# A decode step with cached attention and an MLP on one core: three w4 pieces behind the last V, three wo buffers, the residual put into the accumulator

## The chip, the cores and the metric

The kernel runs on one core of a Trainium2 chip. The core has five engines with their own instruction queues: TensorE (PE, with its weight loads shown as PEld), VectorE (DVE), ScalarE (ACT), GpSimd (POOL) and SyncE (SP), which here issues nearly all loads. Sixteen DMA engines carry each load together. The metric is the device time of one execution in microseconds, the median of three runs. All times below are microseconds (us) unless marked ns; times within the profile count from the start of its span.

## The reference, cut to what matters

One token for each of four sequences passes through two branches that share a layernorm, and both are added to the input:

```
xn  = layernorm(x)                                 # x: 4 x 1 x 576
A   = softmax(q k^T / sqrt(128)) v, then @ wo      # q = xn @ wq, 32 heads of 128;
                                                   # 16 KV heads, the last 2048 of 8192 positions
h   = gelu(layernorm(xn) @ w1), shifted by tokens, @ w2
x1  = xn + that                                    # S = 1: the shifts leave only zeros
B   = x1 + gelu(layernorm(x1) @ w3) @ w4           # w3: 576 x 4608, w4: 4608 x 576
out = x + A + B
```

With one token each shift moves the only row out, so w1 and w2 drop out and x1 is xn. The result is `x + xn + attention @ wo + gelu(...) @ w4`, 4 rows of 576 numbers in bf16. The core has to read 16 K heads and 16 V heads (2 MB each), wq, wo, w3 and w4: 87.17 MB in all.

## The kernel before, in words

**The stages.** First the queries are computed from wq and laid out in `qz`. Then a loop over the 16 K heads (`k_scores`, L251): DVE transposes the head in two instructions (L257), PE multiplies (L266). Beside the first five heads run the pieces of w3 (`g_piece`, L375); then `gelu` makes `gT`, 36 chunks of activations. `softmax` (L272) makes the exponentials `E`, the scaled rows `pr` and their transposes `PZ`. Then a loop over the 16 V heads: `v_compute` (L318) is 64 matmuls on one head, `head_out` (L341) copies the result (`on`, L346) and leaves two things for later: `select` (four small matmuls, L350, and two copies `onx`, L358), and for every second head `project`, which multiplies with one wo tile.

**The accumulator.** `ACC` is one PSUM bank, zeroed at the start by DVE (L180). Columns 0 to 287 gather the sum of all wo and w4 products; the 576 output columns are folded in two halves that stand in partitions 0 to 3 and 32 to 35. `acc_matmuls` (L327) adds one chunk as a pair of matmuls, one for each half. A wo tile is 4 such pairs, a w4 piece of 9 rows is 9 pairs. Columns 320 to 463 hold the w3 product. At the end one DVE instruction adds `xres`, the residual x + xn in the same fold, and casts (`fin`, L458); two small DMAs, on SP's and ACT's queue, write the output (L460).

**What sets the order.** Tiles come from pools with a fixed number of buffers, and a load waits until the buffer's last reader is done: 6 buffers for K and V heads (`kv`), 3 for wq, w3 and w4 (`w`), 2 for wo. All loads stand on SP's queue in the order of the program, so a load that waits holds up every load behind it. A load also waits for the transfer eight places ahead of it to land, since there are eight semaphores for transfers in turn. SP's order after K15, where w4(e, i) is the piece of half e that starts at chunk i:

```
before: w4(0,0) V0 wo0 w4(0,9) V1 w4(1,0) V2 wo1 V3 V4 wo2 V5 V6 wo3 ... V13 V14 wo7 V15 w4(1,9) in 4, 2, 2, 1
```

Each wo tile from wo2 on waits for a projection that frees its buffer (wo2 for that of wo0). On PE the three w4 pieces loaded early are multiplied before, within and after the softmax; the last one, w4(1,9), is split in loads of 4, 2, 2 and 1 chunks, and its products come after V15's.

Of the kernel before, what the change touches and what calls it, by code (L numbers as in the profile page):

```python
# [9 lines left out]
ALU = mybir.AluOpType  # L10
AX = mybir.AxisListType
BF16 = mybir.dt.bfloat16
F32 = mybir.dt.float32
# [8 lines left out]
def kernel(  # L22
# [18 lines left out]
    nc = tc.nc  # L41
    P = 128
    B, Sq, D = A_x.shape
    _, Hkv, Sk, Dh = A_k_cache.shape
# [7 lines left out]
    NCH = W // G  # L52
    NG = P // G
    GK = G // B
# [8 lines left out]
    DH = D // 2  # L63
# [19 lines left out]
    const = ctx.enter_context(tc.tile_pool(name="const", bufs=1))  # L83
# [2 lines left out]
    ktp = ctx.enter_context(tc.tile_pool(name="kt", bufs=2))  # L86
    pzp = ctx.enter_context(tc.tile_pool(name="pz", bufs=1))
    wpl = ctx.enter_context(tc.tile_pool(name="w", bufs=NWP))
    wop = ctx.enter_context(tc.tile_pool(name="wo", bufs=2))
    ps_tp = ctx.enter_context(tc.tile_pool(name="ps_tp", bufs=1, space=PSUM))  # L90
    ps_s = ctx.enter_context(tc.tile_pool(name="ps_s", bufs=4, space=PSUM))
    ps_o = ctx.enter_context(tc.tile_pool(name="ps_o", bufs=2, space=PSUM))
# [34 lines left out]
    ident = const.tile([P, P], BF16)  # L127
# [27 lines left out]
    def transposed_pe(prep):  # L155
        src_bf, dup, T = prep
        tp = ps_tp.tile([P, KJ + 2, B], BF16, tag="tp")
        for j in range(KJ):
            nc.tensor.transpose(out=tp[:, j, :], in_=src_bf[:, j:KJ * P:KJ], identity=ident[0:B, 0:B])
        for e in range(2):  # L160
            nc.tensor.transpose(out=tp[:, KJ + e, :], in_=dup[:, e, :], identity=ident[0:B, 0:B])
        nc.vector.tensor_copy(out=T[:], in_=tp[:])
# [14 lines left out]
        nc.vector.memset(qz_f[:, i * nq:(i + 1) * nq], 0.0)  # L177

    ACC = ps_acc.tile([P, 512], F32)
    nc.vector.memset(ACC[:], 0.0)  # L180
    GP0 = 320
    gp = ACC[:, GP0:GP0 + NF * B].rearrange("p (f b) -> p f b", b=B)
    gT = const.tile([P, NF, B], BF16)
# [39 lines left out]
    for y in range(NY):  # L223
        tq = ps_o.tile([P, 2 * HB, P], BF16, tag="O", name=f"tq{y}")
        for k in range(2):
            for m in range(HB):
                nc.tensor.transpose(out=tq[:, k * HB + m, :],
                                    in_=q_rows[:, k, m, y, :, :].rearrange("p g i -> p (g i)"), identity=ident[:])
# [11 lines left out]
    ln2T = ln2_prep[2]  # L240
    xsum = const.tile([B, D], F32)
    nc.vector.tensor_tensor(out=xsum[:], in0=xn_f[:], in1=x_bf[:], op=ALU.add)
    xres = const.tile([P, DH], F32)
    nc.gpsimd.memset(xres[:], 0.0)
    for q in range(2):
        nc.vector.tensor_copy(out=xres[32 * q:32 * q + B, :], in_=xsum[:, q * DH:(q + 1) * DH])
    transposed_pe(ln2_prep)

    S = []
# [20 lines left out]
                                     skip_group_check=True)  # L270

    def softmax():  # L272
        E = const.tile([P, NCH, NG, GK], F32)
        mx = const.tile([P, NG], F32)
        nb = const.tile([P, 1], F32)
        sm = const.tile([P, NG], F32)
        for g in range(NG):
            nc.vector.reduce_max(out=mx[:, g:g + 1], in_=S[g][:], axis=AX.X)  # L278
        nc.vector.reduce_max(out=nb[:], in_=mx[:], axis=AX.X)
        nc.vector.tensor_scalar_mul(out=nb[:], in0=nb[:], scalar1=-scale)  # L280
        for g in range(NG):
            nc.scalar.activation(out=E[:, :, g, :].rearrange("p (c l) k -> p c k l", l=2),  # L282
                                 in_=S[g][:].rearrange("p (c k l) -> p c k l", k=GK, l=2), func=ACT.Exp, bias=nb[:], scale=scale, accum_out=sm[:, g:g + 1])
        rd = const.tile([P, 1], F32)
        nc.vector.tensor_reduce(out=rd[:], in_=sm[:], op=ALU.add, axis=AX.X)
        nc.vector.reciprocal(out=rd[:], in_=rd[:])
        rdm = const.tile([P, B], F32)
        nc.vector.tensor_scalar_mul(out=rdm[:], in0=mask[:], scalar1=rd[:])  # L288

        PZ = pzp.tile([P, NCH, P], BF16, tag="pz", name="PZ")  # L290
        HC = CP // 2
        for piece in range(NP):
            c0 = piece * CP
            pr = ktp.tile([P, CP, NG, GK, B], BF16, tag="kt", name=f"pr{piece}")
            for b in range(B):
                src = E[:, c0:c0 + CP, :, :].rearrange("p c g k -> p (c g k)")
                dst = pr[:, :, :, :, b].rearrange("p c g k -> p (c g k)")
                if b == 3 or (b == 1 and piece % 2):
                    nc.scalar.mul(out=dst, in_=src, mul=rdm[:, b:b + 1])  # L299
                else:  # L300
                    nc.vector.tensor_scalar_mul(out=dst, in0=src, scalar1=rdm[:, b:b + 1])  # L301
            for half in range(2):
                tp = ps_s.tile([P, HC, P], BF16, tag="S", name=f"pt{piece}{half}")
                for cc in range(HC):
                    nc.tensor.transpose(out=tp[:, cc, :],  # L305
                                        in_=pr[:, half * HC + cc, :, :, :].rearrange("p g k b -> p (g k b)"),
                                        identity=ident[:])
                dst = PZ[:, c0 + half * HC:c0 + (half + 1) * HC, :].rearrange("p c n -> p (c n)")
                src = tp[:].rearrange("p c n -> p (c n)")
                if half:  # L310
                    nc.scalar.copy(out=dst, in_=src)
                else:
                    nc.vector.tensor_copy(out=dst.bitcast(I32), in_=src.bitcast(I32))
        return PZ
# [12 lines left out]
    def acc_matmuls(lhsT, rhs_cols):  # L327
        for q in range(2):
            nc.tensor.matmul(out=ACC[32 * q:32 * q + B, 0:DH], lhsT=lhsT, rhs=rhs_cols(q * DH, (q + 1) * DH),  # L329
                             start=False, stop=False, skip_group_check=True)  # L330
# [4 lines left out]
    def load_wo(g2):  # L335
        wo_tiles[g2] = wop.tile([P, XR, D], BF16, tag="wo", name=f"wo{g2}")
        nc.sync.dma_start(out=wo_tiles[g2][:].rearrange("p x n -> p (x n)"), in_=wo_src[:, g2, :])
# [3 lines left out]
    def head_out(h):  # L341


        O, T = O_tiles.pop(h)
        on = small.tile([P, rep, B], BF16, tag="on")
        nc.vector.tensor_copy(out=on[:].rearrange("p r b -> p b r"), in_=O)  # L346

        def select():
            for x in range(XR):
                nc.tensor.matmul(out=T[0:32, x, :], lhsT=ident[:, x:P:XR], rhs=on[:].rearrange("p r b -> p (r b)"),  # L350
                                 start=(x == 0), stop=(x == XR - 1), skip_group_check=True)
            g2, odd = divmod(h, 2)
            if not odd:
                onx_tiles[g2] = small.tile([P, XR, B], BF16, tag="onx", name=f"onx{g2}")
            onx = onx_tiles[g2]
            for r in range(rep):
                q = 32 * (2 * odd + r)
                nc.vector.tensor_copy(out=onx[q:q + 32, :, :], in_=T[0:32, :, r * B:(r + 1) * B])  # L358
            if odd:
                wt = wo_tiles.pop(g2)  # L360
                onx_tiles.pop(g2)

                def project():
                    for x in range(XR):
                        acc_matmuls(onx[:, x, :], lambda a, z, x=x: wt[:, x, a:z])
                later.append(project)
        later.append(select)

    def run_later():
        fns = later[:]  # L370
        later.clear()
        for fn in fns:
            fn()
# [21 lines left out]
    def load_w4(e, i0, n, cuts):  # L395
        t = wpl.tile([P, n, D], BF16, tag="w", name=f"w4_{e}_{i0}")
        parts = []
        a = 0
        for m in cuts:
            nc.sync.dma_start(out=t[:, a:a + m, :], in_=w4_src[e, :, i0 + a:i0 + a + m, :])  # L400
            parts.append((t[:, a:a + m, :], e, i0 + a, m))
            a += m
        assert a == n
        return parts

    def mlp_out(t, e, i0, n):
        for i in range(n):
            acc_matmuls(gT[:, e * NFH + i0 + i, :], lambda a, z, i=i: t[:, i, a:z])
# [14 lines left out]
                gelu()  # L423


    NV0 = 3
    w4 = []
    for v in range(NV0):
        w4 += load_w4(*((0, 0), (0, 9), (1, 0))[v], 9, (9,))
        V_tiles[v] = kv_load(v_win, v)  # L430
        if v % 2 == 0:
            load_wo(v // 2)
    for part in w4:
        mlp_out(*part)
    PZ = softmax()
    for v in range(Hkv):
        n = v + NV0
        if n < Hkv:
            V_tiles[n] = kv_load(v_win, n)
        if n < Hkv and n % 2 == 0:  # L440
            load_wo(n // 2)
        if n == Hkv:
            end = load_w4(1, 9, 9, (4, 2, 2, 1))
        run_later()
        v_compute(v)
        head_out(v)
    mlp_out(*end[0])
    run_later()
    mlp_out(*end[1])
    while later:  # L450
        run_later()
    for part in end[2:]:
        mlp_out(*part)
    assert not K_tiles and not V_tiles and not wo_tiles

    fin = const.tile([P, DH], out.dtype)
    NR = 32 + B
    nc.vector.tensor_tensor(out=fin[0:NR, :], in0=ACC[0:NR, 0:DH], in1=xres[0:NR, :], op=ALU.add)  # L458
    for q, eng in ((0, nc.sync), (1, nc.scalar)):
        eng.dma_start(out=o2[:, q * DH:(q + 1) * DH], in_=fin[32 * q:32 * q + B, :])  # L460

# [29 lines left out]
```

## Time and profile before

| | |
|---|---|
| median of 3 runs | 219.61 us (219.09 to 219.75) |
| the profiled execution | 219.43 us |
| its span, first to last instruction | 217.5 us |
| mean granted TensorE clock | 0.662 |
| PE, DVE, ACT busy in the span | 115.2, 108.9, 20.9 us |
| read from HBM | 87.17 MB |
| a K head, from issue to landing, median | 24.7 us |
| a V head, from issue to landing, median | 18.5 us |
| an L324 matmul (128x8), mean | 169 ns, x1024 |
| an L329 matmul (128x288), mean | 437 ns on wo, 427 ns on w4 |

The profile divides the span into 40 slices of 5.4 us; a digit is the busy share in tenths. The chain is followed back from the last instruction to what released it at each step. A duration of a matmul includes its way through a pipeline, so several overlap, and the distance between starts tells the rate. "Clock" is the share of TensorE's full clock that was granted. A window row gives length, then for PE, PEld, DVE, ACT and POOL the busy time with the number of instructions, and then the clock, the DMA share and GB/s.

### The profile page before, as it was taken

What the parts mean: (1) busy time and instruction counts of PE and PEld (TensorE: products, weight loads), DVE (VectorE), ACT (ScalarE), POOL (GpSimd) and SP (SyncE); (2) the same over time, 40 slices, a digit from 0 to 9 for tenths busy, and PEclk for the clock granted to TensorE, in tenths of its full rate; (3) what the DMA queues carried; (4) which work ended last, traced back from release to release, by engine and by line L of the source; (5) the groups of instructions that cost most, each with busy time, mean ns of one, the idle gap of its engine ahead of it and who ended that gap; (6) DMA issues with size and microseconds to landing.
All of it is one profiled execution on the core that took longest, in us unless ns stands there. A gap on an engine that the chain in (4) does not pass through costs nothing.

```text
span 217.5 us, 5529 instructions
## 1 busy us (share of the span) xinstructions
PE 115.2 (53%) x2576; PEld 74.9 (34%) x2576; DVE 108.9 (50%) x156; ACT 20.9 (10%) x36; POOL 2.1 (1%) x9
## 2 busy tenths in 40 slices
PE   0243788848444444544452287985626363535453
PEld 0110745517211111111111267874525243434352
DVE  7932968485998998999674754110000000000000
ACT  0202220000000000000005857000000000000000
POOL 1000000000000000000000000000000000000000
PEclk9999999655766855858558566585555555555558
DMA  6999999999999999999999999999999999999950
GB/s 251 428 423 444 412 441 419 413 425 434 420 425 431 422 422 425 431 416 431 428 417 423 430 424 417 410 368 419 419 431 429 419 420 433 409 431 425 412 217 1
DMA packets 8254, 87.52 MB, mean 402 GB/s; under 512 B 924, under 2 KB 1064, under 8 KB 2728
## 3 DMA queue, kind: packets, MB, share of 16 engines
q1 hardware_dynamic: 8216, 87.17, 95.4%
q8 instruction: 20, 0.33, 0.6%
q14 instruction: 2, 0.02, 0.0%
q10 hardware_dynamic: 16, 0.01, 0.0%
HBM read 87.17 MB, written 0.00 MB: 401 GB/s over the span
## 4 chain that ended last, share of the span: by engine, by line
DMA 63%; PE 15%; DVE 14%; ACT 4%; issue 2%; SPq 1%; DVEq 0%; ACTq 0%
DMA t<-in_A_k_cache_dram 36%; DMA t<-in_A_v_cache_dram 24%; DVE kt L257 6%; PE ACC L329 6%; PE O L324 5%; DMA wq<-in_A_wq_dram 3%; ACT E L282 2%; PE pt L305 2%; DVE qz L177 2%; PE qp L201 1%; ACT pr L299 1%; DVE mx L278 1%; DVE pr L301 1%; PE O L350 1%; PE S L266 1%
## 5 line engine op out<-in xcount | busy, mean ns | idle before, releaser
L257 DVE STREAM_TRANSPOSE kt<-t 128x2048 int32<-128x2048 int32 x32 | 72.3, 2292 | 12.5 <-DMA t<-in_A_k_cache_dram 12.5
L266 PE MATMUL S<-kt,qz 32*32 32x512 bf16 x1024 | 36.9, 625 | 37.8 <-DVE kt L257 36.4
L324 PE MATMUL O<-PZ,t 128*128 128x8 bf16 x1024 | 30.2, 169 | 26.6 <-DMA t<-in_A_v_cache_dram 26.0
L324 PEld LDWEIGHTS <-t 128*128 128x128 bf16 x1024 | 28.7, 103 | 31.0 <-DMA t<-in_A_v_cache_dram 29.3
L346 DVE CAST on<-O 128x8 bf16<-128x8 f32 x16 | 2.7, 167 | 61.7 <-PE O L324 61.7
L266 PEld LDWEIGHTS <-qz 32*32 32x32 bf16 x1024 | 10.7, 95 | 60.4 <-issue 57.3
L305 PE MATMUL pt<-ident,pr 128*128 128x128 bf16 x64 | 6.4, 281 | 9.4 <-DVE pr L301 8.4
L382 PEld LDWEIGHTS <-w 128*128 128x128 bf16 x144 | 9.3, 163 | 5.2 <-DMA w<-in_B_w_dram 2.7
L329 PE MATMUL ACC<-wo,onx 128*4 128x288 bf16 x64 | 9.2, 437 | 2.6 <-DVE onx L358 2.6
L382 PE MATMUL ACC<-ln2T,w 128*128 128x4 bf16 x144 | 9.6, 202 | 1.8 <-DMA w<-in_B_w_dram 1.8
L282 ACT ACTIVATE E<-S,nb 128x512 f32<-128x512 f32 x4 | 4.0, 1114 | 59.4 <-DVE nb L280 59.4
L329 PE MATMUL ACC<-w,gT 128*4 128x288 bf16 x72 | 9.4, 427 | 0.0
L305 PEld LDWEIGHTS <-pr 128*128 128x128 bf16 x64 | 5.6, 130 | 10.3 <-ACT pr L299 9.9
L358 DVE CAST onx<-O 32x16 bf16<-32x16 f32 x32 | 5.3, 165 | 6.5 <-PE O L350 6.1
L299 ACT ACTIVATE pr<-E,rdm 128x512 bf16<-128x512 f32 x6 | 7.8, 1422 | 0.7 <-DVE rdm L288 0.7
L301 DVE TENSOR_SCALAR pr<-E,rdm 128x512 bf16<-128x512 f32 x10 | 6.5, 795 | 2.6 <-PE pt L305 2.6
L350 PE MATMUL O<-on,ident 128*32 128x8 bf16 x64 | 4.2, 172 | 4.8 <-DVE on L346 3.3
L201 PE MATMUL qp<-wq,xnT 128*4 128x512 bf16 x32 | 4.0, 621 | 4.4 <-DMA wq<-in_A_wq_dram 4.4
L329 PEld LDWEIGHTS <-gT 128*4 128x4 bf16 x72 | 5.3, 116 | 2.8 <-issue 1.0
L221 DVE CAST q_rows<-qp 128x256 bf16<-128x256 f32 x8 | 2.9, 410 | 6.4 <-PE qp L201 6.3
L350 PEld LDWEIGHTS <-ident 128*32 128x32 bf16 x64 | 4.3, 111 | 4.7 <-issue 4.4
L329 PEld LDWEIGHTS <-onx 128*4 128x4 bf16 x64 | 3.8, 110 | 4.7 <-DVE onx L358 3.1
(66 smaller groups left out, 50.5 us busy)
## 6 DMA issues: line engine op xcount, KB each, us to landing
t<-in_A_k_cache_dram SPq DMA_DIRECT2D x16, 2048.0 KB, 24.7
t<-in_A_v_cache_dram SPq DMA_DIRECT2D x16, 2048.0 KB, 18.5
w<-in_B_w_dram SPq DMA_DIRECT2D x4, 1152.0 KB, 13.0
wo<-in_A_wo_dram SPq DMA_DIRECT2D x8, 576.0 KB, 13.6
wq<-in_A_wq_dram SPq DMA_DIRECT2D x4, 1024.0 KB, 6.0
w<-in_B_w_dram SPq DMA_DIRECT2D x3, 1296.0 KB, 32.5
w_t<-in_B_w_dram SPq DMA_DIRECT2D x1, 576.0 KB, 14.1
w<-in_B_w_dram SPq DMA_DIRECT2D x1, 576.0 KB, 19.0
```

The costliest lines, as they stand in the source:

```text
L201: nc.tensor.matmul(out=qp[k][32 * i:32 * i + B, :], lhsT=lhsT, rhs=rhs, start=False, stop=False, skip_group_check=True)
L257: nc.vector.transpose(out=ap32(kt, e * G * 2, [[2 * G * 2, NCH // 2], [1, 2], [2, G]]), in_=ap32(kn, e * G, [[2 * 2 * G, NCH // 2], [2 * G ...
L266: nc.tensor.matmul(out=S[g][32 * b:32 * b + 32, :].rearrange("p (c k l) -> p c k l", k=GK, l=2), lhsT=qz[32 * g:32 * g + 32, b, h, y, :], ...
L282: nc.scalar.activation(out=E[:, :, g, :].rearrange("p (c l) k -> p c k l", l=2), in_=S[g][:].rearrange("p (c k l) -> p c k l", k=GK, l=2), ...
L299: nc.scalar.mul(out=dst, in_=src, mul=rdm[:, b:b + 1])
L301: nc.vector.tensor_scalar_mul(out=dst, in0=src, scalar1=rdm[:, b:b + 1])
L305: nc.tensor.transpose(out=tp[:, cc, :], in_=pr[:, half * HC + cc, :, :, :].rearrange("p g k b -> p (g k b)"), identity=ident[:])
L324: nc.tensor.matmul(out=O, lhsT=vn[:, c, :], rhs=PZ[:, c, :].rearrange("p (b n) -> p b n", b=B)[:, :, h * rep:(h + 1) * rep], start=(c == 0 ...
L329: nc.tensor.matmul(out=ACC[32 * q:32 * q + B, 0:DH], lhsT=lhsT, rhs=rhs_cols(q * DH, (q + 1) * DH), start=False, stop=False, skip_group_ch ...
L350: nc.tensor.matmul(out=T[0:32, x, :], lhsT=ident[:, x:P:XR], rhs=on[:].rearrange("p r b -> p (r b)"), start=(x == 0), stop=(x == XR - 1), ...
L358: nc.vector.tensor_copy(out=onx[q:q + 32, :, :], in_=T[0:32, :, r * B:(r + 1) * B])
L382: nc.tensor.matmul(out=gp[:, fc, :], lhsT=lhsT, rhs=rhs, start=False, stop=False, skip_group_check=True)
```

## The change

1. Only w4(0,0) is still loaded ahead of the V heads. w4(0,9) and w4(1,0) join w4(1,9) behind V15. Four V heads instead of three are asked for ahead of the softmax.
2. wo has three buffers. wo0 and wo1 stand behind V3, wo2 behind V4, and wo3, wo4 and so on stand behind V6, V8 and so on.
3. SP's order after K15 becomes

```
after:  w4(0,0) V0 V1 V2 V3 wo0 wo1 V4 wo2 V5 V6 wo3 V7 V8 wo4 ... V13 V14 wo7 V15 w4(0,9) w4(1,0) w4(1,9) in 4, 2, 2, 1
```

4. On PE, V15's selection is followed by w4(0,9), the projection of wo7, w4(1,0) and the four parts of w4(1,9).
5. ACC is zeroed by a matmul of the identity with a tile of zeros (`start=True`), and the residual is copied into ACC at the beginning. At the end no sum is left: DVE copies the first 144 columns to `fin` and ScalarE the other 144. `xres` and its memset are gone.
6. `E` moves from its own place into a `w` buffer, which makes room for the third wo buffer.

```diff
-    wop = ctx.enter_context(tc.tile_pool(name="wo", bufs=2))
+    wop = ctx.enter_context(tc.tile_pool(name="wo", bufs=3))
...
-    nc.vector.memset(ACC[:], 0.0)
+    zeros = const.tile([P, 512], BF16)
+    nc.vector.memset(zeros[:], 0.0)
+    nc.tensor.matmul(out=ACC[:], lhsT=ident[:], rhs=zeros[:], start=True, stop=False, skip_group_check=True)
...
-    xres = const.tile([P, DH], F32)
-    nc.gpsimd.memset(xres[:], 0.0)
     for q in range(2):
-        nc.vector.tensor_copy(out=xres[32 * q:32 * q + B, :], in_=xsum[:, q * DH:(q + 1) * DH])
+        nc.vector.tensor_copy(out=ACC[32 * q:32 * q + B, 0:DH], in_=xsum[:, q * DH:(q + 1) * DH])
...
-        E = const.tile([P, NCH, NG, GK], F32)
+        E = wpl.tile([P, NCH, NG, GK], F32, tag="w", name="E")
...
-    NV0 = 3
-    w4 = []
+    NV0 = 4
+    w4 = load_w4(0, 0, 9, (9,))
     for v in range(NV0):
-        w4 += load_w4(*((0, 0), (0, 9), (1, 0))[v], 9, (9,))
         V_tiles[v] = kv_load(v_win, v)
-        if v % 2 == 0:
-            load_wo(v // 2)
-    for part in w4:
-        mlp_out(*part)
+    for g2 in range(2):
+        load_wo(g2)
+    mlp_out(*w4[0])
     PZ = softmax()
     for v in range(Hkv):
         n = v + NV0
         if n < Hkv:
             V_tiles[n] = kv_load(v_win, n)
-        if n < Hkv and n % 2 == 0:
-            load_wo(n // 2)
-        if n == Hkv:
-            end = load_w4(1, 9, 9, (4, 2, 2, 1))
+            if n % 2 == 0:
+                load_wo(n // 2)
         run_later()
         v_compute(v)
         head_out(v)
+    end = load_w4(0, 9, 9, (9,)) + load_w4(1, 0, 9, (9,)) + load_w4(1, 9, 9, (4, 2, 2, 1))
+    run_later()
     mlp_out(*end[0])
-    run_later()
-    mlp_out(*end[1])
     while later:
         run_later()
-    for part in end[2:]:
+    for part in end[1:]:
         mlp_out(*part)
...
-    nc.vector.tensor_tensor(out=fin[0:NR, :], in0=ACC[0:NR, 0:DH], in1=xres[0:NR, :], op=ALU.add)
+    HH = DH // 2
+    nc.vector.tensor_copy(out=fin[0:NR, 0:HH], in_=ACC[0:NR, 0:HH])
+    nc.scalar.copy(out=fin[0:NR, HH:DH], in_=ACC[0:NR, HH:DH])
```

## The prediction

> **What bounds the kernel now.** I read the page's slices first, then the queue table, the chain that ended last, and one-microsecond windows at the two places where the DMA share falls.
>
> ```profile
> span 217.5 us, 5529 instructions
> ...
> DMA  6999999999999999999999999999999999999950
> ...
> q1 hardware_dynamic: 8216, 87.17, 95.4%
> q8 instruction: 20, 0.33, 0.6%
> ...
> DMA 63%; PE 15%; DVE 14%; ACT 4%; issue 2%; SPq 1%; DVEq 0%; ACTq 0%
> ```
>
> The DMA engines are busy in every slice but the first and the last two, no other engine is over 53%, and transfers hold 63% of the chain. 87.17 MB have to come in; the change moves none of them away. So only three things can give time: idle time of the DMA engines, what PE, DVE and the output copy do after the last bytes, and the start. The windows:
>
> ```profile
> 138.00:140.00 2.00, 2.00 (x24) 1.79 (x23) 0.66 (x4) 0.00 (x0) 0.00 (x0) 0.50 0.94 401
> 140.00:141.00 1.00, 1.00 (x12) 0.74 (x8) 0.00 (x0) 0.00 (x0) 0.00 (x0) 0.50 0.91 377
> 141.00:142.00 1.00, 1.00 (x29) 0.69 (x26) 0.00 (x0) 0.00 (x0) 0.00 (x0) 0.50 0.46 180
> 142.00:143.00 1.00, 1.00 (x45) 1.00 (x42) 0.00 (x0) 0.00 (x0) 0.00 (x0) 0.82 0.78 249
> ...
> 209.00:210.00 1.00, 1.00 (x44) 1.00 (x42) 0.00 (x0) 0.00 (x0) 0.00 (x0) 0.50 0.52 197
> 210.00:211.00 1.00, 0.74 (x27) 0.73 (x25) 0.17 (x1) 0.00 (x0) 0.00 (x0) 0.50 0.38 129
> 211.00:212.00 1.00, 1.00 (x12) 0.90 (x9) 0.33 (x2) 0.00 (x0) 0.00 (x0) 0.50 0.05 18
> ```
>
> The last columns are granted clock, DMA share and GB/s. There is a gap at 141 to 143, and at the end the share falls in steps over 3 us: the 16 engines do not finish together. The end of the chain and of the timeline:
>
> ```profile
> 190.45 18.15 DMA t<-in_A_v_cache_dram
> 208.59 0.05 issue
> 208.64 1.89 PE O L324 x64
> ...
> 211.95 0.93 PEld L329 LDWEIGHTS <-onx 128*4 128x4 bf16 x8
> 212.19 1.25 PE L329 MATMUL ACC<-wo,onx 128*4 128x288 bf16 x8
> 212.91 0.69 PEld L329 LDWEIGHTS <-gT 128*4 128x4 bf16 x6
> 213.15 1.01 PE L329 MATMUL ACC<-w,gT 128*4 128x288 bf16 x6
> 214.21 0.45 DVE L458 TENSOR_TENSOR fin<-ACC,xres 36x288 bf16<-36x288 f32 x1 [2.80 <-PE ACC L329]
> ```
>
> V15 has landed at 208.59. Then come its 64 matmuls, the selection, 26 matmuls into ACC, and DVE at 214.21: 5.6 us. The last w4 piece is issued at 192.6 and takes 19.2 us, so it lands at 211.8, 2.4 us ahead of DVE.
>
> **Part 1: the gap.** Every transfer raises its semaphore 16 times, once per DMA engine. From these events: V4 finishes at 141.44 on the first engine and 144.69 on the last; wo2, which is issued at 141.42 after waiting for wo0's projection, finishes at 144.58 on the first and 146.09 on the last. A wo takes 1.40 us (144.69 to 146.09 on the last engine, so that one did not idle). The first engine idled 144.58 - 1.40 - 141.44 = 1.74 us. After the change, 15.7 MB stand behind K15 up to V5, as now up to V4. Next is V6, which waits for V0's product. That ends at 137.5 now and, with one w4 group of 2.3 us (125.0 to 127.2) gone from the middle of the softmax, near 135.3. A load flows 1.76 us after its issue (141.42 to 143.18), so the first engines need it issued by 139.7: 4 us of cover. wo3 behind it, with V7 in its queue, waits for wo0's projection, which in the built order follows V3's product, near 142; V6 itself lasts the first engines until 146.3. The gap closes.
>
> What is it worth? The spread between first and last engine grows by 1.28 us in one step at K15 (1.84 to 3.12), just when one of the 20 instruction blocks of 16 KB is fetched (102.7). In the landing events eight engines fall back by such steps, one after the other and then again, and the others never do. The last engine had no idle time at the gap, so filling the gap hurries the first engines only. The stream still ends at 211.8 on the last one, and I value this part at **0**. If all engines gained, it would be 1.74.
>
> The Trainium skill ("Runtime: NRT & Kernel Launch", Instruction fetch mechanics) says that crossing a 16 KiB block costs one bump of a DMA tail, "mostly hidden". The 1.28 us step disagrees, for the data behind the block; by that rule the engines would stay level, and the sum would be 1.74 us lower.
>
> **Part 2: w4 behind V15.** Two pieces of 1296 KB move from before V1 and V2 to behind V15; such a piece takes 3.1 us (wo0 landed at 117.37, the next w4 piece at 120.48). With the end fixed at 211.8, landings run backwards from it with today's spacings: the last pieces at 211.81, 211.44, 210.70, 210.00; w4(1,0) 1.41 earlier at 208.59; w4(0,9) at 205.48; V15 at 202.4 instead of 208.59. V15's product, selection and the copies end near 205.1, hidden under the next piece.
>
> What is left for PE is 9 pairs for w4(0,9), 4 for wo7, 9 for w4(1,0), then 4, 2, 2 and 1: 31 pairs. The two matmuls of a pair run side by side; in the trace pairs start every 0.240 us at clock 0.50. At that rate PE, starting at 205.55, is never out of work: the last pair starts 30 x 0.24 later at 212.75 and ends about 0.53 on, with DVE at 213.3. That is 0.9 better than 214.21.
>
> But the clock moves. The granted share is 0.5 or 1.0 in stretches of multiples of 3.41 us, with edges at 142.36 and 214.04. Both follow about 3 us of such pairs: 138.0 to 141.3, and 210.8 to 214. In the group at 113.57 the clock rises at 115.06 and pairs go from 0.240 to 0.120 us apart. The V products alone (1.9 us in 4.9) never raise it from 145.8 to 208. On today's grid the edges are 207.21 and 210.63; the window before the second is full of pairs. Any other phase puts the edge at 208 to 211.5. About 21 pairs are done by 210.63; the rest take 0.12, and the last piece decides: 211.81 + 0.05, then 0.29 for one pair at full clock and 0.05 to DVE: **212.2, a gain of 2.0**. With the latest edge it is 212.65.
>
> **Part 3: the end.** The sum of 0.448 us (36x288) becomes two copies of 36x144. In the built program ScalarE's copy waits for the count that the DVE copy itself raises, so they run one after the other. DVE: between 0.167 (128x8) and 0.410 (128x256), 0.28; a 128x144 copy took 0.266. ScalarE: between 0.188 (128x32) and 0.375 (128x256), 0.28. Hop: 0.09 from L280's end to L282, I take 0.07. Together 0.63 instead of 0.448: **+0.19** (0.12 to 0.28). ScalarE has loaded its table once already (1.28 us, at q_rows), and copies after its exponentials needed none.
>
> The Trainium skill ("PSUM — Partial Sum Buffer", PSUM bank collisions raise a hardware error) lets no two engines touch one bank and 32-partition quadrant at once, reads included. No run here shows a collision. By it the halves cannot overlap; if they could, part 3 would be about -0.15.
>
> **Part 4: the start.** DVE's memset of ACC (0.485 us) becomes one of half the words (0.24), PE gets one 512-column matmul (0.6 at most, L201's mean), xres and its memset on POOL go, and two 0.29 us copies write PSUM instead of SBUF (0.2 to 0.4). All hide under the first loads: PE frees wq's buffer at 11.4, and queued bytes last until 14.1. Cost 0; if that cover of 2.7 us were gone, up to 0.5. E moves into a w buffer whose last tenant, a w3 piece, is read near 50 us; the w4 loads take buffers that are free before the last V's are asked for. Cost 0, at most 0.2.
>
> **Sum.** 0 - 2.0 + 0.19 + 0 = -1.8: span 215.7, and with the 1.9 us around it (219.43 - 217.5) 217.6. The profiled execution is 0.18 below the median of 219.61, so **217.8**. This measurement can tell about 0.3%, 0.66 us, from no change.
>
> **Rivals.**
> - *Half clock to the end.* No edge falls in the pairs: 213.3 + 0.19, so -0.7: 218.9, on the edge of what can be told. Against it: the three bursts above. Chance 0.15.
> - *The gap pays.* All engines gain up to 1.74, on top of the sum: 216.1. For: 1.25 us of bytes are missing there. Against: the last engine's 1.40 for wo2. Chance 0.10.
> - *A block more on a late engine.* Fetches follow PE's program, which the change shifts by 72 instructions in the V stage. One more block on the last engine costs 1.28: 219.1. Chance 0.11.
> - *Slower: V6's wait.* V6, not V5, now stands first behind a V product. The last engines run dry at 144.7, so from an issue at 142.9 every microsecond late costs one; from 144.7 on the kernel is slower than before. V0's product would have to end 7 us later than it does now. At an issue of 146, 220.9. Chance 0.05.
> - The forecast: 0.59.
>
> The rival on the end copy, parallel halves, is inside the range. Low end: the gap half paid, 216.9; high end: the block case, 219.2. Both outer rests hold under 2 in 10. Faster: 0.59 + 0.10 + half of 0.15 + 0.02 of the block case: 0.79; same 0.16; slower 0.05.
>
> **What would show it.** No dip at 141 to 143; V6 issued near 135 to 137; the last w4 landing still near 211.8 with the spread of the engines at 4.4 us rather than 2.8; the clock rising to 1.0 between 208 and 211.5; PE waiting for the last small w4 piece; DVE's copy, then ScalarE's, 0.6 us in all. It is wrong if the last landing moves by more than 0.5 us, or if the pairs stay 0.24 apart.

## The result and the profile after

The changed kernel takes 217.66 us (median of 4 runs, 217.53 to 217.78) against 219.48 for the kernel before in the same series. The ratio is 0.9918, with a 95% interval of 0.9901 to 0.9936: faster by 0.8%. The forecast was 217.8. Two later series of the same kernel gave 0.9899 (0.9874 to 0.9924) and 0.9897 (0.9871 to 0.9923). The profiled execution took 217.53, its span is 215.8. A ratio leaves out slow runs, those over 1.5% above the fastest of their kernel, while a median counts them; e6, e8 and e9 have such runs, and the traces of e6 and e9 are of such runs.

The page of the changed kernel: span, clock and DMA in 40 slices, and the queues.

```profile
span 215.8 us, 5535 instructions
...
PEclk9999999658566665678578566555555555555559
DMA  6999999999999999999999999999999999999960
...
q1 hardware_dynamic: 8216, 87.17, 96.0%
q8 instruction: 20, 0.33, 0.6%
```

The same bytes, the same 20 instruction blocks, and as before nearly every slice full. Windows of the changed kernel at the former gap and at the end (length, five engines, clock, DMA share, GB/s; a DMA packet counts whole in the window in which it starts, so a share can pass 1):

```profile
140.00:141.00 1.00, 0.58 (x22) 0.52 (x20) 0.00 (x0) 0.00 (x0) 0.00 (x0) 0.50 0.99 410
141.00:142.00 1.00, 0.00 (x0) 0.00 (x0) 0.00 (x0) 0.00 (x0) 0.00 (x0) 0.50 0.99 410
142.00:143.00 1.00, 0.41 (x10) 0.42 (x10) 0.10 (x1) 0.00 (x0) 0.00 (x0) 0.50 1.12 475
...
209.00:210.00 1.00, 1.00 (x12) 0.57 (x10) 0.00 (x0) 0.00 (x0) 0.00 (x0) 0.50 0.47 168
210.00:211.00 1.00, 1.00 (x20) 0.68 (x18) 0.00 (x0) 0.00 (x0) 0.00 (x0) 0.97 0.25 82
211.00:212.00 1.00, 0.78 (x14) 0.34 (x8) 0.00 (x0) 0.00 (x0) 0.00 (x0) 1.00 0.06 20
```

The gap is closed: 410 GB/s at 141 to 142, where it was 180. At the end the share falls over a longer stretch than before, and the clock rises at 210. The counts in brackets also hold matmuls still under way from the window before: from 209 to 210 eight matmuls of L330 start, from 210 to 211 sixteen. The timeline of the changed kernel at its end:

```profile
205.63 2.32 PE L330 MATMUL ACC<-w,gT 128*4 128x288 bf16 x18 [0.72 <-DMA w<-in_B_w_dram]
207.74 1.17 PE L330 MATMUL ACC<-wo,onx 128*4 128x288 bf16 x8
208.73 2.64 PE L330 MATMUL ACC<-w,gT 128*4 128x288 bf16 x30
211.59 0.67 PE L330 MATMUL ACC<-w,gT 128*4 128x288 bf16 x6 [0.22 <-DMA w<-in_B_w_dram]
212.30 0.30 DVE L456 CAST fin<-ACC 36x144 bf16<-36x144 f32 x1 [7.00 <-PE ACC L330]
212.63 0.27 ACT L457 CAST fin<-ACC 36x144 bf16<-36x144 f32 x1 [77.41 <-DVE fin L456]
212.93 0.35 SPq L459 DMA_DIRECT2D out_dram<-fin  x1
```

The last six matmuls wait for a load, as forecast: the stream of bytes now ends the kernel, not the work behind V15. ScalarE's copy starts when DVE's ends. From the landing events, one increment per DMA engine, the last w4 piece finishes at 207.00 on the first engine and at 211.92 on the last; before it was 208.99 and 211.81. So the first engines gained 2.0 us, the last ones nothing.

### The profile page after: what moved, and what is told of

The parts are those of the page before. It is cut to its first block, busy times and chain, and to the rows that moved or that the text cites. A ratio compares the mean times of both kernels' runs of the same rounds, so it can differ in the third digit from the quotient of the medians.

```text
span 215.8 us, 5535 instructions
## 1 busy us (share of the span) xinstructions
PE 114.9 (53%) x2577; PEld 74.2 (34%) x2577; DVE 108.7 (50%) x156; ACT 21.3 (10%) x37; POOL 1.8 (1%) x8
## 4 chain that ended last, share of the span: by engine, by line
DMA 70%; DVE 13%; PE 7%; ACT 5%; issue 3%; SPq 1%; DVEq 0%; ACTq 0%
DMA t<-in_A_k_cache_dram 36%; DMA t<-in_A_v_cache_dram 21%; DMA w<-in_B_w_dram 9%; DVE kt L258 6%; DMA wq<-in_A_wq_dram 3%; PE O L325 2%; ACT E L283 2%; PE pt L306 2%; ACT pr L300 2%; DVE qz L177 2%; PE qp L204 1%; ACT PZ L312 1%; DVE mx L279 1%; DVE pr L302 1%; PE ACC L330 1%
## 5 line engine op out<-in xcount | busy, mean ns | idle before, releaser
L330 PE MATMUL ACC<-wo,onx 128*4 128x288 bf16 x64 | 9.0, 437 | 2.2 <-DVE onx L359 2.2
L330 PE MATMUL ACC<-w,gT 128*4 128x288 bf16 x72 | 7.3, 362 | 0.9 <-DMA w<-in_B_w_dram 0.9
L330 PEld LDWEIGHTS <-gT 128*4 128x4 bf16 x72 | 3.9, 103 | 4.7 <-issue 2.2
```

## The experiments

Each ratio is against the kernel before on the same chip in the same series, with its 95% interval. The runs of e6 and e9 scatter by nearly 2%, so their traces are read for the order of events and for steps, not for small differences of time.

### e1: the gap alone

```diff
-    wop = ctx.enter_context(tc.tile_pool(name="wo", bufs=2))
+    wop = ctx.enter_context(tc.tile_pool(name="wo", bufs=3))
...
-        E = const.tile([P, NCH, NG, GK], F32)
+        E = wpl.tile([P, NCH, NG, GK], F32, tag="w", name="E")
```
(on the kernel before)

> The kernel before with three wo buffers and E in a w buffer, and nothing else: wo2 no longer waits for wo0's projection, so the dip of the DMA share at 141 to 143 closes. The theory (the last of the 16 engines never idled there, so filling the gap only hurries the others): last V15 landing stays near 208.6, spread of the engines at the end rises from 2.8 to about 4.5 us, time 219.5, ratio 1.000 within 0.002. The rival (the gap pays): V15 lands 1.2 to 1.7 us earlier, time 217.8 to 218.3, ratio 0.992 to 0.994.

Measured: 219.34 us, ratio 0.9988 (0.9976 to 1.0000). Windows and the end of e1:

```profile
141.00:142.00 1.00, 0.69 (x18) 0.63 (x18) 0.77 (x5) 0.00 (x0) 0.00 (x0) 0.50 0.99 402
142.00:143.00 1.00, 1.00 (x44) 1.00 (x41) 0.00 (x0) 0.00 (x0) 0.00 (x0) 0.50 1.10 448
```

```profile
208.47 1.87 PE L324 MATMUL O<-PZ,t 128*128 128x8 bf16 x64 [3.96 <-DMA t<-in_A_v_cache_dram]
...
214.04 0.45 DVE L458 TENSOR_TENSOR fin<-ACC,xres 36x288 bf16<-36x288 f32 x1 [2.80 <-PE ACC L329]
```

The gap is gone (0.99 where it was 0.46), yet V15's product starts at 208.47 instead of 208.64. The last landing is 211.62, the spread between the engines 4.75 us instead of 2.82. This is what the theory expected: filling the gap hurried only the engines that were ahead. At most 0.24% is in it.

### e2: the w4 pieces alone

```diff
-    w4 = []
+    w4 = load_w4(0, 0, 9, (9,))
     for v in range(NV0):
-        w4 += load_w4(*((0, 0), (0, 9), (1, 0))[v], 9, (9,))
...
+    end = load_w4(0, 9, 9, (9,)) + load_w4(1, 0, 9, (9,)) + load_w4(1, 9, 9, (4, 2, 2, 1))
```
(on the kernel before: two wo buffers, xres and the sum stay; products in the changed order)

> The kernel before with the three w4 pieces behind V15 and nothing else: two wo buffers, wo2 behind V4 waiting for wo0's projection, the sum with xres at the end in one DVE instruction. 2.65 MB fewer now stand ahead of wo2, 6.2 us. The first engines run dry near 135, the last near 138.5. The theory: if the projection of wo0 frees wo2 near 139, the last engines lose up to 2 us, so of the 2.0 us gained in the tail 0 to 2 are lost: 217.5 to 219.5; if wo2 is freed only after V3's product near 142, they lose about 5 us and the kernel is slower than before, 221 to 223. The rival (the third buffer is worth nothing, only w4's place counts): 217.5 with the last landing at 211.8.

Measured: 223.18 us, ratio 1.0141 (1.0103 to 1.0180): slower than before, and a little more than the 221 to 223 expected for a late wo2. Windows of e2, whose trace is of the slowest of six runs (223.99):

```profile
136.00:138.00 2.00, 1.38 (x30) 1.04 (x28) 0.97 (x6) 0.00 (x0) 0.00 (x0) 0.50 0.18 74
138.00:140.00 2.00, 2.00 (x61) 1.74 (x60) 0.17 (x1) 0.00 (x0) 0.00 (x0) 0.50 0.00 0
140.00:141.00 1.00, 1.00 (x30) 0.78 (x25) 0.33 (x2) 0.00 (x0) 0.00 (x0) 0.50 0.00 0
```

All 16 engines stand still for three microseconds, since the queue ahead of wo2 is 6.2 us shorter and wo2 is issued only at 140.53. Now the last engines idle too: V4 lands on the last at 138.63 and wo2 at 144.23, where 1.40 would do, so 4.2 us are lost. The last landing moved by more, from 211.81 to 218.56: behind the stall the spread between the engines grew from 0.66 to 4.2 us, where before the change it grew from 1.51 to 2.82. Why it grew so much more is not shown. So the third wo buffer has no worth of its own that the runs can tell (e1), and without it the move of w4 costs more than it brings.

### e3: one copy at the end, and the changed kernel beside it

```diff
-    nc.vector.tensor_copy(out=fin[0:NR, 0:HH], in_=ACC[0:NR, 0:HH])
-    nc.scalar.copy(out=fin[0:NR, HH:DH], in_=ACC[0:NR, HH:DH])
+    nc.vector.tensor_copy(out=fin[0:NR, :], in_=ACC[0:NR, 0:DH])
```
(on the changed kernel)

> The changed kernel with one DVE copy of 36x288 at the end in place of the two halves. The theory (the halves run one after the other, 0.30 + 0.03 + 0.27 us): one copy takes 0.41 to 0.45, so 0.15 to 0.2 us less than the changed kernel, 217.5, ratio to before 0.991. The rival (the halves were worth it): 0.1 to 0.2 us more, 217.8.

> The changed kernel with one DVE copy at the end, once more, beside the changed kernel on the same chip: 0.15 to 0.2 us less than that, 217.45.

> The changed kernel once more, on the same chip as the three runs beside it: 217.6, ratio to before 0.991.

Measured: 217.41 (0.9902, 0.9883 to 0.9921) in the first series; in the second 217.61 (0.9910, 0.9880 to 0.9939) beside 217.44 (0.9897, 0.9871 to 0.9923) for the changed kernel. The whole kernel can't tell the two apart. Only the profile does. The end of the second e3 run:

```profile
212.18 0.45 DVE L455 CAST fin<-ACC 36x288 bf16<-36x288 f32 x1 [7.08 <-PE ACC L330]
212.66 0.35 SPq L457 DMA_DIRECT2D out_dram<-fin  x1
```

From DVE's start to the issue of the output it is 0.48 us with one copy and 0.63 with two. The split costs 0.15 us at its place; that the time falls by as much is not shown.

### e10: the order alone

```diff
     (on the kernel before: the new order of loads and products, three wo buffers, E in a w buffer;
      the memset of ACC, xres and the final sum stay)
```

> The kernel before with the new order of loads and products, three wo buffers and E in a w buffer; ACC is still zeroed by DVE, xres stays, and one DVE sum of 36x288 ends it. The theory: all of the gain is in the order, and the sum takes 0.45 us as one copy does: as the changed kernel with one copy, 217.4, ratio 0.990. If zeroing by a matmul or the residual in ACC were worth something at the start, this would be slower than e3 by that much.

Measured: 217.39 us, ratio 0.9889 (0.9863 to 0.9915), in the same series as the second e3 run and the third of the changed kernel. The end of e10:

```profile
212.23 0.45 DVE L454 TENSOR_TENSOR fin<-ACC,xres 36x288 bf16<-36x288 f32 x1 [7.08 <-PE ACC L329]
212.71 0.35 SPq L456 DMA_DIRECT2D out_dram<-fin  x1
```

The whole gain is there with the old start and the old sum. A sum of two operands takes the same 0.45 us as a copy of that size. So zeroing by a matmul, the residual in ACC and the two copies bring nothing that could be measured.

### e4: two pieces behind V15 instead of three

```diff
-    w4 = load_w4(0, 0, 9, (9,))
+    w4 = load_w4(0, 0, 9, (9,)) + load_w4(0, 9, 9, (9,))
...
-    end = load_w4(0, 9, 9, (9,)) + load_w4(1, 0, 9, (9,)) + ...
+    end = load_w4(1, 0, 9, (9,)) + ...
```
(on the changed kernel)

> The changed kernel with w4(0,9) loaded early again, behind w4(0,0): two pieces behind V15 instead of three. The theory (the stream ends at 211.9 either way, and PE's work behind V15's landing decides): V15 lands near 205.6, its product and selection end near 208.4, then 22 pairs; at half clock until an edge of the clock between 210 and 213, so DVE starts at 212.6 to 213.6 instead of 212.3: 218.0 to 219.0. The rival (any number of pieces behind V15 hides the product): as the changed kernel, 217.7.

Measured: 218.73 us, ratio 0.9948 (0.9923 to 0.9972). The end of e4:

```profile
210.62 1.17 PE L330 MATMUL ACC<-wo,onx 128*4 128x288 bf16 x8
211.58 2.13 PE L330 MATMUL ACC<-w,gT 128*4 128x288 bf16 x18
213.75 0.30 DVE L457 CAST fin<-ACC 36x144 bf16<-36x144 f32 x1 [5.57 <-PE ACC L330]
```

The last landing is 211.70, as with three pieces, but DVE starts at 213.75. V15 lands at 205.36, 2.9 us later than in the changed kernel, and PE's pairs start at 208.50 instead of 205.63. The clock stays at 0.50 until 213.33, so nearly all 22 pairs ran 0.24 apart. So one piece fewer costs 0.3 to 0.5%, by the three series of the changed kernel: the rows behind V15 hide its product, and an early start of the pairs also brings the clock up in time. This is the half-clock rival, seen where the pairs start too late.

### e5, e6 and e9: the length of PE's program

```diff
e5 -        for c in range(NCH):
e5 +        for c in range(0, NCH, 2):
e6 +        for c in [c for _ in range(2 if h < 12 else 1) for c in range(NCH)]:
e9 +        if 0 < h < 14:
e9 +            for _ in range(60):
e9 +                nc.tensor.matmul(out=S[0][0:32, 0:8], lhsT=zeros[0:32, 0:32], rhs=zeros[0:32, 0:8],
e9 +                                 start=False, stop=False, skip_group_check=True)
```
(each on the changed kernel; e5 and e6 in `v_compute`, e9 at the end of `k_scores`; e5 also moves the mark of the sum's end to the last matmul left)

> The changed kernel with every second matmul of the V products left out, so half of each V head isn't summed; all loads stay. PE's program has 1024 instructions less, 4 blocks of 16 KB. The theory (the fetches of these blocks make eight of the 16 engines late, 1.28 us each): 16 blocks instead of 20, so no engine is hit a third time; spread at the last landing 3.3 to 3.6 us instead of 4.9, last landing near 210.5 instead of 211.9, time 216.1 to 216.5. The rival (the lateness has nothing to do with the program's length): spread 4.9, last landing 211.9, time 217.6.

> The changed kernel with the 64 matmuls of V heads 0 to 11 done twice, the second time over the first; heads 12 to 15, all loads and the end stay. PE's program has 1536 instructions more, 6 blocks of 16 KB. The theory: 26 blocks, so some engines are hit a fourth time before the end; spread at the last landing 6.0 to 6.3 us instead of 4.9, last landing near 213.2, time 218.8 to 219.2. The rival: spread 4.9 and 217.6, since PE has about 3 us to spare at each V head and 1.9 us more of work there hides.

> The changed kernel with 60 more matmuls of 32x8 after each of the K heads 1 to 13, zeros times zeros added to the scores, so the result stays. PE's program has 1560 instructions more, 6 blocks of 16 KB; they stand in the K stage, where PE waits for DVE, and the V stage stays as it is. The theory (each block makes one of eight engines late by 1.28 us, in turn): 26 blocks, so the first engines are hit a fourth time; spread at the last landing 6.0 to 6.3 us, last landing near 213.2, time 218.7 to 219.2. The rival (the lateness has another cause): spread 4.9, last landing 211.9, time 217.6.

e5 measured 216.65 us, ratio 0.9845 (0.9811 to 0.9880). The spread at the last landing is 4.00 us and the last landing 210.86, so 1.06 us earlier than in the changed kernel. One engine stands 0.6 us behind the next four (3.3 to 3.4): the 8 KB block fetched at 55.2 fell on an engine that already had one of 16 KB (spread 2.05 at K4, 2.58 at K5). The forecasts of 3.3 to 3.6 us of spread and of 216.1 to 216.5 us missed that. In six traces of the changed order with all of its matmuls, the changed kernel's three, e3's two and e10's, the spread is 4.53 to 5.36 and the last landing 211.81 to 212.78, so e5 lies outside of both.

e6 and e9 were slower, 230.35 (1.0447, 1.0397 to 1.0496) and 224.67 (1.0198, 1.0153 to 1.0242), and not for the reason that they were made for. In e6 V6 was issued at 137.4, but wo3 behind it only at 153.5, since wo0's projection had to wait behind products that took twice as long and behind two waits of PE, 2.2 and 2.7 us, each at the fetch of a block. In e9 PE had 60 more matmuls for each of 13 K heads and stood still for 1.8 to 3.0 us at each of eleven blocks up to 124 us; the scores, the softmax and V0's product came later by both. PE and SP in e9:

```profile
147.29 0.57 PE L329 MATMUL O<-PZ,t 128*128 128x8 bf16 x16 [0.60 <-ACT PZ L316]
```

```profile
119.23 28.98 SPq L100 DMA_DIRECT2D t<-in_A_v_cache_dram  x2
154.39 0.33 SPq L342 DMA_DIRECT2D wo<-in_A_wo_dram  x1
```

The row that starts at 119.23 holds V5 and V6: V6 is issued when V0's product is done, near 147.7. V6 then lands on the first engine at 154.60, 13.2 us after V5, and on the last at 155.16, 8.6 us after V5, where 4.9 would do: 3.7 us are lost there. This is the slower rival of the prediction, V6's wait, come true at an issue 5 us past its limit.

So neither run shows what a fourth block on one engine costs at the end. But up to the stall e9 answers the question by its steps. Times of the 9th and 17th instruction block, and the transfer at whose landing the spread jumps:

```
                 9th block        spread            17th block       spread
before           102.7            K15: 1.84 to 3.12  183.4           V11: 2.41 to 2.84 (after the gap)
changed          102.8            K15: 1.94 to 3.27  176.6           V11: 3.46 to 4.78
e1               103.2            K15: 1.92 to 3.17  182.0           V11: 3.50 to 4.75
e5               103.5            K15: 2.61 to 3.47  none (16 blocks)  4.0 to 4.2 from V5 on
e9                83.1            K11: 2.13 to 3.67  144.0           V5:  3.72 to 5.23
```

In e9 the blocks come earlier, because the program is longer ahead of that point, and the jumps come earlier with them, at other transfers. Where there is no 17th block there is no such jump. That engines fall back because of the fetches is therefore shown. The events don't name the engines; that eight of them fall back in turn is read from the sorted times, where eight of 16 step back once before any steps back twice. (In e5 the first step is smaller because one engine was already at 2.6.) The packet records give part of the price: a fetch of 16 KB takes 1.02 to 1.11 us in the changed kernel, a row of a V head of the same size 0.61 in the median. Why the fetch is slower, and where the rest of the 1.3 to 1.5 us comes from, is not shown.

### e8: an attempt to level the engines

```diff
...
+        cuts = (0, 16, 24, 32) if split else (0, 32)
+        for p0, p1 in zip(cuts[:-1], cuts[1:]):
+            nc.sync.dma_start(out=dst[B * p0:B * p1, :], in_=src[p0:p1])
...
```
(on e3, for V8 alone)

> The changed kernel with one copy at the end, and V8 loaded in three transfers, of 64, 32 and 32 rows of 16 KB. The Trainium skill (DMA: Bandwidth & Descriptors, Why a DMA increments its semaphore by 16 and not by 1) says that a transfer whose slowest dimension has 8 steps runs on the eight lowest-numbered engines; the two of 32 rows have 8 steps there. If that holds, eight engines get 12 rows of V8 and the others 4, instead of 8 each: a shift of 4 rows, 2.45 us, from one half to the other. If the late engines are the ones that get less, the spread at the last landing falls from 4.9 to 2.5 to 3.5 us, the last landing comes 1.0 to 1.5 us earlier and the time is 216.2 to 216.8. If the late engines get more, the spread grows to 9.8 and the time is 219.5 to 220.5. If all engines share it, as e3, 217.4.

Measured: 227.05 us, ratio 1.0293 (1.0248 to 1.0338), worse than any of the three cases. Slices of e8:

```profile
GB/s 259 442 410 448 400 430 428 434 420 421 421 423 429 426 432 418 421 435 413 440 429 423 410 427 431 416 425 272 214 218 366 420 427 420 429 418 427 407 255 13
```

From about 151 to 168 the core loads at half its rate, far longer than the 4.9 us that two transfers on eight engines would take. The landing events do show that each of the two small transfers finished on eight engines only. The packet records add that packets took about twice as long: in steps of 2 us from 154 to 168 the median packet of 16 KB takes 1.07 to 1.27 us instead of 0.61, and the DMA share, which adds up the packets' times, stays at 0.90 to 1.14. So the rate did not fall for want of packets at work. Which engines carried them, and whether the small transfers, the narrower target or something else made them slow, stays open.

### after_again

> The changed kernel once more, on the chip of these runs: 217.4 to 217.9, ratio to before 0.991 to 0.993.

Measured: 217.63 us, ratio 0.9899 (0.9874 to 0.9924).

## Why the prediction was right, step by step

- **Part 1, the gap: right.** It closed, V6 was issued at 135.66, and closing it alone is worth 0.0 to 0.24% (e1). The reason was right too: the last engines had no idle time there, and they are late because instruction blocks fall on them (e5, e9). The spread was sized too small, 4.92 us against 4.4. I had taken 1.28 us, the step at the ninth block, for every further one; from the ninth to the sixteenth the eight late engines fell back by 1.5 us on average (from 1.77 to 3.28 us behind the first engine, K14 to wo5).
- **A cover in part 1 was far thinner than stated.** I put wo0's projection near 142 and saw more than 2 us to spare. It ended at 144.39. The chain of the changed kernel shows why:

```profile
139.04 1.53 PE O L325 x54
140.58 1.87 issue
142.45 0.42 PE O L325 x10
```

PE stands still for 1.87 us inside V3's product, with its operands there. The fetch of an instruction block had begun at 140.08, 2.37 us before PE went on. This is no chance meeting: the 14 traces hold 32 stretches of more than 0.5 us in which PE waits for nothing that the profile shows, and each ends 2.3 to 2.6 us after the fetch of a 16 KB block began. wo3 landed 1.50 us behind V6 on the first engine, where 1.40 is the least, so the cover was used up and that engine idled for 0.1 us. In the first e3 trace, with wo3 issued at 145.47, it idled for 0.7. The last engine lost nothing either time (1.41 and 1.39), so this miss cost nothing.
- **Part 2, w4 behind V15: right in each term.** V15 landed at 202.47 (202.4 was forecast), the next two pieces at 205.59 and 208.69 (205.48, 208.59), the last at 211.92 (211.81). The clock rose at 210.06 (208 to 211.5). DVE started at 212.30 instead of 214.21: 1.91 us of gain, 2.0 forecast. The step rested on the clock. In the five other traces of this order (the changed kernel's, e3's and e10's) it rose at 209.00 to 211.16, so the rise did not hang on one lucky phase; in e4, where the pairs start 2.9 us later, it came too late.
- **Part 3, the end: right in sign and size.** 0.63 us from DVE's start to the issue instead of 0.47, so +0.16, where 0.19 was forecast. The second copy follows the first, as the forecast had read in the program.
- **Part 4, the start: right as far as can be told.** e10 has the old start and is as fast.
- **The sum**: span 215.8 against 215.7.
- **The rivals.** The gap does not pay (e1). Half clock to the end did not come about here, but does in e4. V6's wait did not come about (135.66 against a limit of 142.9), but does in e9. A further block on a late engine before the end was not seen: the changed kernel has 20 blocks, as before.

The Trainium skill ("Runtime: NRT & Kernel Launch", Instruction fetch mechanics) calls the cost of crossing a block of 16 KiB "mostly hidden". For PE the changed kernel's trace agrees but for one block of 20, which cost 1.87 us; in e9 eleven of 26 cost 1.8 to 3.0 us each. The section does not speak of the data on the same DMA engine, which falls back by 1.3 to 1.5 us with each block. So the 1.28 us step adds to the page rather than disagreeing with it, and the engines that "stay level" are the prediction's inference, not the page's.

No version that forms the whole result beats the changed kernel by more than the runs can tell (e5 leaves out half of each V head's sum). e10, which has only the new order, is as fast (0.9889 against 0.9897 in the same series) and is the simpler kernel.

## What to carry to other kernels

Where loads bound a kernel, look at the landing of a transfer on the last DMA engine, not at the mean DMA share: a gap that only the other engines had was worth nothing that could be measured when it was filled (e1). Put bytes whose use is short behind the bytes whose use is long, and check that what keeps the queue full still does when those bytes have left the front: e2 made the same move without the third buffer and lost 1.4%. Before splitting a final copy over two engines, read which semaphore the second half waits for.

## What the runs showed of the hardware that was not expected

- Instruction blocks of 16 KB make single DMA engines late by 1.3 to 1.5 us each, eight of the 16 in turn; after 20 blocks the last engine was 4.9 us behind the first, 2.3% of the span.
- PE can run out of instructions while its data is there: for 1.87 us in the changed kernel, for up to 3.0 in e9, until 2.3 to 2.6 us after the fetch of a block began.
- Matmuls of 8 columns did not raise the clock, however closely they came: in e6 PE ran them from 155.84 to 162.54 with one pause of 0.25 us, and the granted clock stayed at 0.50.
- Splitting one V head into loads of 64, 32 and 32 rows brought the rate down to 214 to 272 GB/s for some 17 us (e8); the cause is open.
